# Attention's second product as 64 by 64 tiles, in batches of eight row groups

## The chip, the cores and the metric

The kernel runs on one core of a Trainium2 chip. The metric is the device time of one execution in microseconds (us), given as a median over runs. TensorE multiplies matrices into PSUM, a memory of eight banks; VectorE (DVE in the profile), ScalarE (ACT) and GpSimd (POOL) do elementwise work, POOL on SBUF alone in this kernel; SyncE (SP) issues most transfers.

## The reference

Two independent parts are computed, and their outputs stand side by side. Part A is a state-space layer (a complex linear recurrence over 2048 steps, with projections before and after). Part B is attention over segments of 32 tokens with a memory of 8 rows:

```python
for s in range(n_seg):                       # 64 segments of 32 tokens
    xs = x[:, s * seg_len:(s + 1) * seg_len, :].copy()
    h = jnp.concatenate([mem, xs], axis=1)   # 8 + 32 rows
    q, k, v = (jnp.einsum('btd,dhe->bhte', h, W) for W in (Wq, Wk, Wv))   # 32 heads of 128
    scores = jnp.einsum('bhqe,bhke->bhqk', q, k) * scale
    scores = jnp.where(mask[None, None], scores, -1000000000.0)
    p = _softmax(scores, axis=-1)
    o = jnp.einsum('bhqk,bhke->bhqe', p, v)
    o = jnp.einsum('bhte,hed->btd', o, Wo)
    mem = o[:, :M, :].copy()
    outs.append(o[:, M:, :])
```

The change is in the line that makes `o` from `p` and `v`, the second product.

## The kernel before

**Stages.** Projections of V and part A's recurrence come first, then part A's output, then the attention of part B (about 466 to 992 us in the profile), then the output projection. The memory rows of all segments are guessed ahead and checked at the end, so that the segments need no order.

**Attention.** The 2048 tokens are 16 groups of 128 rows, four segments in each. The 32 heads are worked in 16 head pairs (`hp`). A head pair has nine units: eight (`u` 0 to 7) of two groups each, and a small one (`NU`) for the first 40 rows with the true memory. At the start of a head pair `scores` computes all scores, transposed (keys on partitions), in 64 by 64 blocks: 64 matmuls of 128x64 tiles (L639) into four PSUM banks, one O buffer of two banks and both S buffers. PSUM is given out under three names of two buffers each: O (two banks a buffer), S and P (one bank a buffer).

`exps` turns one bank of scores into probabilities on ScalarE (L652). For each unit `att_front` multiplies two 64 by 64 blocks of each group by the causal mask on POOL (L663) into `mx`, a buffer of 128x128 tiles whose other blocks stay zero. Two units later `att_back` runs a quartet of matmuls, two groups by two heads (L704): the whole 128x128 tile of `mx` is the stationary operand and 129 columns of V (128 and a column of ones, which gives the sum of the softmax) move. VectorE adds the memory rows' share `b_u` (L706) and takes reciprocals (L708); POOL multiplies (L712) into `b_ot`, and after four units SP stores `b_ot` to DRAM in rows of 256 elements (L719, L720).

**What lies between.** Projections of Q and K for later head pairs fill TensorE: a head pair has 18 steps of `proj`, 16 of eight matmuls with 480 columns (L582) and two of sixteen with 136 (L593), with their casts on VectorE (L78) or ScalarE (L76). The main loop runs two steps a unit, 19 steps ahead. In the last head pair no projections are left, and steps of the output projection (`early`, L760) stand in. In the first head pairs, steps of `v_mem` project the memory rows' values (L484 on TensorE, sums at L511).

**What sets the order.** TensorE's order in attention follows the program, in which a unit, its projections and its exps are written out in `kernel_main`; the other engines' orders come from the compiled program, and PSUM buffers rotate, so that a matmul waits until the reader of its buffer two uses ago is done. SP's queue is in order: a store that waits for POOL holds back the loads behind it. V and `b_u` of a half (eight groups) are loaded into one of three buffers, about one head pair ahead (L606, L619).

Of the kernel before, what the change touches and what calls it, by code (L numbers as in the profile page):

```python
# [9 lines left out]
FP32 = mybir.dt.float32  # L10
# [3 lines left out]
ALU = mybir.AluOpType  # L14
# [79 lines left out]
def masks(k):  # L94

    G = k.G
    k.maskX = k.cst.tile([128, 128], BF16, name="maskX")
    k.maskM = k.cst.tile([128, L], BF16, name="maskM")
    G.memset(k.maskX[:], 0.0)
    G.memset(k.maskM[:], 0.0)  # L100
    for j in range(4):
        r = slice(32 * j, 32 * j + 32)
        G.memset(k.maskX[r, r], 1.0)
        G.affine_select(out=k.maskX[r, r], in_=k.maskX[r, r], compare_op=ALU.is_ge, fill=0.0, base=0,
                        pattern=[[1, 32]], channel_multiplier=-1)
    m = k.maskM[0:L, :]
    G.memset(m, 1.0)
    G.affine_select(out=m, in_=m, compare_op=ALU.is_ge, fill=0.0, base=0, pattern=[[1, L]], channel_multiplier=-1)
    G.memset(k.maskM[0:L, 0:M], 1.0)
# [185 lines left out]
class PartB:  # L295
# [219 lines left out]
    def qk_init(self, pool):  # L515
# [22 lines left out]
        for c in (0, VW - 1):  # L538
            G.memset(self.vs[:, :, c:c + 1], 1.0)
        self.ms = []  # L540
        self.mx, self.es, self.todo = [], {}, []
        for i in range(4):
            t = pool.tile([128, 4, 128], BF16, name=f"b_mx{i}", bufs=1)
            G.memset(t[:], 0.0)
            self.mx.append(t)
        for i in range(2):
            t = pool.tile([128, 2, 128], BF16, name=f"b_ms{i}", bufs=1)
            G.memset(t[:], 0.0)
# [62 lines left out]
    def load_u(self, i):  # L611
        if i < 2 * HP:
            k = self.k
            hp, half = divmod(i, 2)
            v = self.vt[hp // 2][:, :]
            for j in range(4):
                r = M - 1 + 32 * half + j
                src = bass.AP(v.tensor, v.offset + r * 512 + (hp % 2) * 256, [[0, 32], [4 * 512, NU], [1, 256]])
                d = k.SP.dma_start(self.ub[i % 3][32 * j:32 * j + 32, :, 1:257], src)  # L619
                if i < 3:  # L620
                    k.tc.keep_in_program_order(d)
# [7 lines left out]
    def scores(self, hp):  # L629
# [5 lines left out]
        for v in range(4):  # L635
            for j in range(8):
                g = M + (4 * v + j // 2) * 128
                for r in (0, 64):
                    k.tc.keep_in_program_order(k.PE.matmul(  # L639
                        banks[v][r:r + 64, j * 64:j * 64 + 64], kt[:, j % 2, g + r:g + r + 64], qt[:, j % 2, g + r:g + r + 64],  # L640
                        start=True, stop=True))
        self.todo = [(hp, v, banks[v]) for v in range(4)]
        self.exps()

    def exps(self):

        if self.todo:
            k = self.k
            hp, v, s = self.todo.pop(0)
            e = self.p3.tile([128, 512], BF16, name="b_e", bufs=4)  # L650
            i = hp * UPH + v
            k.S.activation(e[:], s, ACT.Exp, scale=float(E) ** -0.5, accum_out=self.accE[:, i:i + 1])  # L652
            self.es[2 * v], self.es[2 * v + 1] = (e[:, 256 * a:256 * a + 256] for a in range(2))

    def att_front(self, hp, u):
        k = self.k; PE = k.PE
        if u < NU:
            if u == 0:
                self.scores(hp)
            m = self.mx[u % 4]  # L660
            e = self.es.pop(u).rearrange("p (j q) -> p j q", j=4)
            for r in (slice(0, 64), slice(64, 128)):
                k.G.tensor_tensor(m[r, :, r], e[r], k.maskX[r, r].unsqueeze(1).to_broadcast([64, 4, 64]), ALU.mult)  # L663
            return m
        qt, kt = self.qk[hp % 2]
        s = k.ps("S")
        i = hp * UPH + u
        for hh in range(2):
            PE.matmul(s[:, hh * L:(hh + 1) * L], kt[:, hh, 0:128], qt[:, hh, 0:L], start=True, stop=True)
        e = self.p3.tile([128, 2 * L], BF16, name="b_es", bufs=1)  # L670
        k.S.activation(e[:], s[:, 0:2 * L], ACT.Exp, scale=float(E) ** -0.5, accum_out=self.accE[:, i:i + 1])
        m = self.ms[hp % 2]
        k.G.tensor_tensor(m[:, :, 0:L], e[:].rearrange("p (j q) -> p j q", j=2), k.maskM[:].unsqueeze(1).to_broadcast([128, 2, L]), ALU.mult)
        return m

    def att_back(self, hp, u, m):
        k = self.k; PE, V = k.PE, k.V
        o = k.ps("O")
        i = hp * UPH + u
        if u == NU:  # L680
            for hh in range(2):
                cs = slice(hh * 129, hh * 129 + 129)
                PE.matmul(o[:, 0, cs], m[:, hh, :], self.vs[:, hp % 2, cs], start=True, stop=True)
            r = self.rall[0:L, 4 * i:4 * i + 2]
            oa = o[0:L, 0, 0:VW]
            V.reciprocal(r, oa[:, 0:VW:VW - 1])
            if hp % 2 == 0:
                self.om = self.p3.tile([L, 2, 256], BF16, name="b_om", bufs=2)
            V.tensor_tensor(self.om[:, hp % 2, :].rearrange("p (h e) -> p h e", h=2), oa[:, 1:257].rearrange("p (h e) -> p h e", h=2),
                            r.unsqueeze(2).to_broadcast([L, 2, E]), ALU.mult)  # L690
            if hp % 2:
                hb = hp // 2
                cs = slice((hb % 2) * 512, (hb % 2) * 512 + 512)
                om = self.om[:].rearrange("p h n -> p (h n)")
                k.SP.dma_start(self.os[hb // 2][0:SEG, cs], om[M:L, :])
                k.SP.dma_start(self.omd[:, hb * 512:hb * 512 + 512], om[0:MT, :])
            return
        half, v = divmod(u, 4)
        b = (2 * hp + half) % 3
        vt, ut = self.vb[b], self.ub[b]  # L700
        for gg in range(2):
            for hh in range(2):
                cs = slice(hh * 129, hh * 129 + 129)
                PE.matmul(o[:, gg, cs], m[:, 2 * gg + hh, :], vt[:, 2 * v + gg, cs], start=True, stop=True)  # L704
        s = self.p3.tile([128, 2, VW], FP32, name="b_s", bufs=3)
        V.tensor_tensor(s[:], o[:, :, 0:VW], ut[:, 2 * v:2 * v + 2, :], ALU.add)  # L706
        r = self.rall[:, 4 * i:4 * i + 4].rearrange("p (a b) -> p a b", a=2)
        V.reciprocal(r, s[:, :, 0:VW:VW - 1])  # L708
        if v == 0:
            self.ot = self.p3.tile([128, NU, 256], BF16, name="b_ot", bufs=3)  # L710
        ot = self.ot
        k.G.tensor_tensor(ot[:, 2 * v:2 * v + 2, :].rearrange("p g (h e) -> p g h e", h=2),  # L712
                          s[:, :, 1:257].rearrange("p g (h e) -> p g h e", h=2),
                          r.unsqueeze(3).to_broadcast([128, 2, 2, E]), ALU.mult)
        if v == 3:
            os = self.os[hp // 4]
            cs = slice((hp % 4) * 256, (hp % 4) * 256 + 256)
            if half == 0:
                k.SP.dma_start(os[SEG:128, cs], ot[SEG:128, 0, :])  # L719
            k.SP.dma_start(os[1024 * half + 128 * (1 - half):1024 * half + 1024, cs].rearrange("(g p) n -> p g n", p=128), ot[:, 1 - half:NU, :])  # L720

    def attention(self):
        units = [(hp, u) for hp in range(HP) for u in (0, 1, 2, 3, NU, 4, 5, 6, 7)]
        pend = []
        for n, (hp, u) in enumerate(units):
            if u == 2:
                self.load_v(2 * hp + 2)
                self.load_u(2 * hp + 2)
            if u == 3 and hp % 2 == 0:
                self.load_vs(hp // 2)  # L730
            if u == 5:
                self.load_v(2 * hp + 3)
                self.load_u(2 * hp + 3)
            pend.append((hp, u, self.att_front(hp, u)))
            if len(pend) > 2:
                self.att_back(*pend.pop(0))
            yield hp, u
        for p in pend:
            self.att_back(*p)
            yield HP, 0  # L740


    def load_o(self, tb, q):
# [200 lines left out]
def kernel_main(tc, A_x, A_Lre, A_Lim, A_Bre, A_Bim, A_Cre, A_Cim, A_logdt, A_Dskip, B_x, B_mem0, B_Wq, B_Wk, B_Wv, B_Wo, out,  # L944
                force=False, dbg=None):
    with ExitStack() as ctx:
# [129 lines left out]
        with pool("p3", "right") as p3:  # L1076
# [19 lines left out]
            b.wo0, b.acc = [], {}  # L1096
            early = chain(b.op_some([(0, 0), (1, 0)], range(3), "P", 2), b.op_some([(2, 0), (3, 0)], range(3), "S", 2))
            for n, (hp, u) in enumerate(at):
                if u in (3, 5, 6) and hp < 7:
                    next(vms[hp + 1])  # L1100
                if u == 4 and hp < 6:
                    next(vms[hp + 2])
                if u == 4 and 8 <= hp < 12:
                    w = k.w8((8, 512), "wo0")
                    k.SP.dma_start(w, b.Wo[:, 8 * (hp - 8):8 * (hp - 7), 0:512])
                    b.wo0.append(w)
                if u == 6 and hp in (4, 8, 12):
                    b.load_o(0, hp // 4 - 1)
                want = min(18 * HP, 19 + 2 * (n + 1))
                if done == want:  # L1110
                    for _ in range(3 if u > 3 else 2):
                        next(early, None)
                for _ in range(2 if done == want else 0):
                    b.exps()
                while done < want:
                    next(pr)
                    b.exps()
                    done += 1
                    if done == 18 * HP:
                        w1 = xep.tile([128, KC, XP], BF16, name="b_xe")  # L1120
                        b.wo1 = w1[:].rearrange("p c n -> p (c n)")[:, 0:H * 512].rearrange("p (h n) -> p h n", h=H)
                        k.SP.dma_start(b.wo1, b.Wo[:, :, 512:D])
            for _ in early:
                pass

# [100 lines left out]
```

## Time and profile before

| what | value |
|---|---|
| median of 3 runs | 1199.17 us (1199.07 to 1200.29) |
| the profiled execution | 1199.58 us, span 1197.9 us |
| TensorE busy | 1192.0 us, 100% of the span |
| VectorE, ScalarE, POOL busy | 584.8, 346.3, 355.2 us |
| L704, second product | 512 matmuls, 51.0 us busy |
| L639, scores | 1024 matmuls |
| L663, masks on POOL | 256 instructions, 170.0 us |
| L706 and L708 on VectorE | 128 each, 88.5 and 22.8 us |
| L712, multiplies on POOL | 128 instructions, 133.0 us |

The granted clock of TensorE was full throughout. Busy times of matmuls overlap each other (each is drawn with its latency), so the time that a group takes from TensorE's stream is read from the starts of neighbours in the timeline. Idle time of other engines costs nothing while TensorE has work.

### The profile page before, as it was taken

The numbers are of one execution on the slowest core, as the hardware profiler recorded it, in microseconds if no ns is written. First come the engines' busy times: TensorE is split into PE (matmuls) and PEld (weight loads), VectorE is DVE, ScalarE is ACT, GpSimd is POOL, SyncE is SP. The second block draws the span as 40 slices with busy tenths as digits, with TensorE's granted clock in tenths as the row PEclk, the third lists the DMA queues.
The fourth block names the chain that finished last, engine by engine and source line by source line (L and its number), as shares of the span: only waits on it lengthen the run. The fifth ranks groups of instructions, "written<-read, shape, count | busy, mean of one in ns | idle before, by whom it ended". The sixth has DMA issues, their size and how long they took to land.

```text
span 1197.9 us, 20039 instructions
## 1 busy us (share of the span) xinstructions
PE 1192.0 (100%) x8104; PEld 608.9 (51%) x8104; DVE 584.8 (49%) x1004; ACT 346.3 (29%) x713; POOL 355.2 (30%) x484
## 2 busy tenths in 40 slices
PE   9999999999999999999999999999999999999998
PEld 4444444444445544555555555555555554444444
DVE  4889999999982333244344444444444432100000
ACT  3344344443420002334433343333333310000000
POOL 1000000000012332355555666666666671000000
PEclk9999999999999999999999999999999999999999
DMA  9941332322656732988789776855585478807000
GB/s 239 269 126 55 96 105 63 97 84 66 148 178 200 230 103 62 222 209 175 179 179 214 174 177 146 175 134 137 136 169 132 98 214 194 202 18 158 18 27 20
DMA packets 333873, 168.50 MB, mean 141 GB/s; under 512 B 144512, under 2 KB 327608, under 8 KB 333760
## 3 DMA queue, kind: packets, MB, share of 16 engines
q1 hardware_dynamic: 331696, 165.33, 56.5%
q10 hardware_dynamic: 2080, 1.84, 0.5%
q8 instruction: 65, 1.06, 0.4%
q14 instruction: 32, 0.26, 0.1%
HBM read 89.74 MB, written 43.70 MB: 111 GB/s over the span
## 4 chain that ended last, share of the span: by engine, by line
PE 98%; POOL 1%; issue 0%; DVE 0%; ACT 0%; POOLq 0%; ACTq 0%
PE psP L582 35%; PE psS L760 10%; PE psS L386 9%; PE psP L386 9%; PE psO L234 9%; PE psS L288 5%; PE psP L288 5%; PE psP L760 4%; PE psP L593 3%; PE psO L704 3%; PE psO L760 2%; PE psS L793 1%; PE psO L639 1%; PE psP L484 1%; POOL b_mx L663 1%; PE psS L639 1%
## 5 line engine op out<-in xcount | busy, mean ns | idle before, releaser
L582 PE MATMUL psP<-b_xe,w 128*128 128x480 bf16 x2048 | 435.9, 366 | 0.0
L582 PEld LDWEIGHTS <-w 128*128 128x128 bf16 x2048 | 194.2, 98 | 186.1
L663 POOL TENSOR_TENSOR b_mx<-b_e,maskX 64x256 bf16<-64x256 bf16 x256 | 170.0, 664 | 96.1 <-ACT b_e L652 53.8
L78 DVE CAST b_q<-psP 128x480 bf16<-128x480 f32 (+2 forms) x160 | 92.2, 585 | 203.5 <-PE psP L582 134.3
L712 POOL TENSOR_TENSOR b_ot<-b_s,b_rall 128x512 bf16<-128x512 f32 x128 | 133.0, 1039 | 118.3 <-DVE b_rall L708 111.5
L283 POOL TENSOR_TENSOR a_xd<-a_xn,b_wide 128x512 f32<-128x512 bf16 x32 | 36.8, 1152 | 418.4 <-DMA a_xn<-in_A_x_dram 350.8
L386 PEld LDWEIGHTS <-b_xe 128*128 128x128 bf16 x1024 | 99.8, 98 | 119.1 <-DVE b_xe L78 0.3
L760 PEld LDWEIGHTS <-b_ol 128*128 128x128 bf16 x960 | 93.4, 98 | 110.3
L76 ACT ACTIVATE b_k<-psP 128x480 bf16<-128x480 f32 x128 | 72.7, 568 | 252.3 <-PE psP L582 248.4
L706 DVE TENSOR_TENSOR b_s<-psO,b_u 128x516 f32<-128x516 f32 x128 | 88.5, 692 | 100.3 <-PE psO L704 81.9
L234 PE MATMUL psO<-w,a_bt 128*128 128x512 bf16 x512 | 115.7, 379 | 0.0
L760 PE MATMUL psS<-w,b_ol 128*128 128x512 bf16 x416 | 92.9, 379 | 0.0
L386 PE MATMUL psS<-w,b_xe 128*128 128x512 bf16 x384 | 90.7, 379 | 0.0
L386 PE MATMUL psP<-w,b_xe 128*128 128x512 bf16 x384 | 90.7, 379 | 0.0
L234 PEld LDWEIGHTS <-a_bt 128*128 128x128 bf16 x512 | 49.7, 98 | 59.0
L288 PEld LDWEIGHTS <-a_hs 128*128 128x128 bf16 x512 | 49.5, 98 | 58.3
L78 DVE CAST b_ost<-psS 128x512 bf16<-128x512 f32 x13 | 9.0, 691 | 138.6 <-PE psS L760 138.6
L565 ACT ACTIVATE b_wide<-w 128x1024 bf16<-128x1024 bf16 x64 | 67.6, 1056 | 0.5
L76 ACT ACTIVATE b_vst<-psS 128x512 bf16<-128x512 f32 x56 | 33.4, 597 | 96.1 <-PE psS L386 80.3
L288 PE MATMUL psS<-w,a_hs 128*128 128x512 bf16 x256 | 57.9, 379 | 0.0
L288 PE MATMUL psP<-w,a_hs 128*128 128x512 bf16 x256 | 57.9, 379 | 0.0
L76 ACT ACTIVATE b_vst<-psP 128x512 bf16<-128x512 f32 x56 | 33.4, 597 | 83.8 <-PE psP L386 77.7
(205 smaller groups left out, 1107.5 us busy)
## 6 DMA issues: line engine op xcount, KB each, us to landing
b_v<-b_vx SPq DMA_DIRECT2D x32, 512.0 KB
b_u<-b_vt SPq DMA_DIRECT2D x128, 128.0 KB
b_vx<-b_vst SPq DMA_DIRECT2D x56, 256.0 KB
w<-in_B_Wv_dram SPq DMA_DIRECT2D x14, 1024.0 KB
w<-in_B_Wo_dram SPq DMA_DIRECT2D x12, 1024.0 KB
w<-in_B_Wq_dram SPq DMA_DIRECT2D x16, 512.0 KB
w<-in_B_Wk_dram SPq DMA_DIRECT2D x16, 512.0 KB
b_os<-b_ot SPq DMA_DIRECT2D x16, 512.0 KB
```

The lines of the kernel that those rows point to most:

```text
L76: self.S.activation(out, in_, ACT.Copy)
L78: self.V.tensor_copy(out, in_)
L234: m = PE.matmul(u[:, i, :], self.bt[:, i, c, :], self.xT[tb][:, c, :], start=(c == 0), stop=(c == KC - 1))
L283: G.tensor_tensor(xd[:], xn[:], dB[:, hs], ALU.mult)
L288: PE.matmul(py[:], self.hs[tb][:, pc, i, tt * 128:(tt + 1) * 128], self.ct[half, i][:, pc, :], start=(pc == 0 and i == 0), stop=(pc == PC ...
L386: m = self.k.PE.matmul(p[:], self.xe[:, c, t * 128:(t + 1) * 128], w[:, c, :], start=(c == 0), stop=(c == KC - 1))
L565: k.tc.keep_in_program_order(k.S.activation(wide, w[:, i * KC:(i + 1) * KC, hh * 128:(hh + 1) * 128], ACT.Square, accum_out=self.nrm[:, n: ...
L582: PE.matmul(p[:, 0:480], w[:, i * KC + c, hh * 128:(hh + 1) * 128], self.xe[:, c, 480 * q:480 * q + 480], start=(c == 0), stop=(c == KC - 1))
L663: k.G.tensor_tensor(m[r, :, r], e[r], k.maskX[r, r].unsqueeze(1).to_broadcast([64, 4, 64]), ALU.mult)
L706: V.tensor_tensor(s[:], o[:, :, 0:VW], ut[:, 2 * v:2 * v + 2, :], ALU.add)
L712: k.G.tensor_tensor(ot[:, 2 * v:2 * v + 2, :].rearrange("p g (h e) -> p g h e", h=2), s[:, :, 1:257].rearrange("p g (h e) -> p g h e", h=2 ...
L760: k.PE.matmul(self.acc[t, half], ol[:, h8, tt * 128:(tt + 1) * 128], self.wo_half(half, h), start=(h == 0), stop=(h == H - 1))
```

## The change

The second product uses 64 by 64 tiles of TensorE, four at a time: two row halves (keys) by two column halves (queries, that is, PSUM partitions). Four groups give the lower 64 output partitions and four the upper, so that eight groups, a half of the sequence, form one batch of 32 matmuls in `values`. It writes six PSUM banks: both O buffers and both S buffers, with the two row halves in different banks. The probabilities stay compact: they are masked in place, one POOL instruction of 128x512 for each bank of scores, and `mx` goes. `norm3` and `norm1` add, take reciprocals and multiply, for six and two blocks of 64 rows at a time; they and the later exps are put in a list, from which `tick` takes one after each projection step. The output rows lie in another order on the partitions, and the store and the load of `b_u` are rearranged to match. The head pair's units run 0 to 8 with the batches in units 3 and 7 and the small unit in 4 and 6; loads and `v_mem` steps move to other units.

```diff
 def masks(k):
-    k.maskX = k.cst.tile([128, 128], BF16, name="maskX")
+    k.maskX = k.cst.tile([128, 64], BF16, name="maskX")
...
     def load_u(self, i):
-                r = M - 1 + 32 * half + j
-                src = bass.AP(v.tensor, v.offset + r * 512 + (hp % 2) * 256, [[0, 32], [4 * 512, NU], [1, 256]])
+                r = M - 1 + 32 * half + 16 * (j // 2) + j % 2
+                src = bass.AP(v.tensor, v.offset + r * 512 + (hp % 2) * 256, [[0, 32], [2 * 512, NU], [1, 256]])
...
     def scores(self, hp):
-        self.todo = [(hp, v, banks[v]) for v in range(4)]
-        self.exps()
+        self.exp(hp, 0, banks[0])
+        self.todo += [(self.exp, hp, v, banks[v]) for v in range(1, 4)]
...
+    def exp(self, hp, v, s):
...
+        k.S.activation(e[:], s, ACT.Exp, scale=float(E) ** -0.5, accum_out=self.accE[:, i:i + 1])
+        ev = self.es[v] = e[:].rearrange("p (j q) -> p j q", j=8)
+        k.G.tensor_tensor(ev, ev, k.maskX[:].unsqueeze(1).to_broadcast([128, 8, 64]), ALU.mult)
...
-            m = self.mx[u % 4]
-            e = self.es.pop(u).rearrange("p (j q) -> p j q", j=4)
-            for r in (slice(0, 64), slice(64, 128)):
-                k.G.tensor_tensor(m[r, :, r], e[r], k.maskX[r, r].unsqueeze(1).to_broadcast([64, 4, 64]), ALU.mult)
...
-        for gg in range(2):
-            for hh in range(2):
-                PE.matmul(o[:, gg, cs], m[:, 2 * gg + hh, :], vt[:, 2 * v + gg, cs], start=True, stop=True)
-        s = self.p3.tile([128, 2, VW], FP32, name="b_s", bufs=3)
-        V.tensor_tensor(s[:], o[:, :, 0:VW], ut[:, 2 * v:2 * v + 2, :], ALU.add)
...
+    def values(self, hp, half):
...
+        vt = self.vb[(2 * hp + half) % 3]
+        o = [k.ps("O") for i in range(2)]
+        sp = [k.ps("S") for i in range(2)]
+        for v, hh in [(v, hh) for hh in range(2) for v in range(3)] + [(3, 0), (3, 1)]:
+            cs = slice(hh * 129, hh * 129 + 129)
+            for i in range(2):
+                e = self.es[2 * half + i]
+                ph = slice(64 * i, 64 * i + 64)
+                for b in range(2):
+                    r = slice(64 * b, 64 * b + 64)
+                    out = sp[b][ph, cs] if v == 3 else o[hh][ph, b, v * 129:v * 129 + 129]
+                    k.tc.keep_in_program_order(k.PE.matmul(
+                        out, e[r, 2 * v + hh, :], vt[r, 4 * i + v, cs], start=True, stop=True))
+        self.ot = self.p3.tile([128, NU, 256], BF16, name="b_ot", bufs=3)
+        self.norm3(hp, half, 0, o[0])
+        self.todo += [(self.norm3, hp, half, 1, o[1]), (self.norm1, hp, half, 0, sp[0]), (self.norm1, hp, half, 1, sp[1])]
...
+    def norm3(self, hp, half, hh, o):
...
+        s = self.p3.tile([128, 2, 3, 129], FP32, name="b_s", bufs=3)
+        k.V.tensor_tensor(s[:], o[:, :, 0:387].rearrange("p b (v n) -> p b v n", v=3),
+                          four(self.ub[(2 * hp + half) % 3])[:, :, :, hh * 129:hh * 129 + 129], ALU.add)
...
+        k.V.reciprocal(r, s[:, :, :, 128 * hh])
+        k.G.tensor_tensor(four(self.ot)[:, :, :, hh * E:hh * E + E], s[:, :, :, 1 - hh:1 - hh + E],
+                          r.unsqueeze(3).to_broadcast([128, 2, 3, E]), ALU.mult)
+    def norm1(self, hp, half, b, sp):
...
+        V.tensor_tensor(s[:, b, :], sp[:, 0:VW], self.ub[(2 * hp + half) % 3][:, 6 + b, :], ALU.add)
+        if b == 0:
+            return
...
+        os = self.os[hp // 4][1024 * half:1024 * half + 1024, (hp % 4) * 256:(hp % 4) * 256 + 256]
+        os = os.rearrange("(i w p) n -> i p w n", i=2, w=NU)
+        if half:
+            k.SP.dma_start(os[0], self.ot[0:64])
+        else:
+            k.SP.dma_start(os[0, SEG:64, 0, :], self.ot[SEG:64, 0, :])
+            k.SP.dma_start(os[0, :, 1:NU, :], self.ot[0:64, 1:NU, :])
+        k.SP.dma_start(os[1], self.ot[64:128])
...
     def attention(self):
-        units = [(hp, u) for hp in range(HP) for u in (0, 1, 2, 3, NU, 4, 5, 6, 7)]
...
+                if u in (3, 7):
+                    self.values(hp, u // 4)
+                if u == 4:
+                    self.small_front(hp)
+                if u == 6:
+                    self.small_back(hp)
+                yield hp, u
...
-                if u in (3, 5, 6) and hp < 7:
+                if u in (2, 4, 6) and hp < 7:
                     next(vms[hp + 1])
...
                 if done == want:
-                    for _ in range(3 if u > 3 else 2):
-                        next(early, None)
+                    for i in range(2):
+                        if i < (2, 1, 0, 2, 1, 2, 0, 2, 2)[u]:
+                            next(early, None)
+                        b.tick()
                 while done < want:
                     next(pr)
-                    b.exps()
+                    b.tick()
```

## Prediction

> **What bounds the kernel now.** I read the page first (engine totals, the chain that ended last), then TensorE's timeline inside one head pair of the attention stage, then the groups by form for the instructions that the change touches, and last the timeline around the one stall.
>
> ```profile
> PE 1192.0 (100%) x8104; PEld 608.9 (51%) x8104; DVE 584.8 (49%) x1004; ACT 346.3 (29%) x713; POOL 355.2 (30%) x484
> PE 98%; POOL 1%; issue 0%; DVE 0%; ACT 0%; POOLq 0%; ACTq 0%
> ```
>
> TensorE is the whole chain, and every other engine is busy half of the span or less. So only two things can move the end: the time that TensorE's own stream takes, and any new wait in that stream. The stream itself, two units of the head pair that starts at 720 us:
>
> ```profile
> 716.22 1.11 PE L593 MATMUL psP<-b_xe,w 128*128 128x136 bf16 x16
> 717.17 0.40 PE L704 MATMUL psO<-b_v,b_mx 128*128 128x129 bf16 x4
> 717.41 1.11 PE L593 MATMUL psP<-b_xe,w 128*128 128x136 bf16 x16
> 718.35 1.78 PE L582 MATMUL psP<-b_xe,w 128*128 128x480 bf16 x8
> 720.07 0.70 PE L639 MATMUL psO<-b_q,b_k 128*64 128x64 bf16 x32
> 720.59 0.67 PE L639 MATMUL psS<-b_q,b_k 128*64 128x64 bf16 x32
> 721.20 0.41 PE L704 MATMUL psO<-b_v,b_mx 128*128 128x129 bf16 x4
> 721.45 3.40 PE L582 MATMUL psP<-b_xe,w 128*128 128x480 bf16 x16
> 724.68 0.40 PE L704 MATMUL psO<-b_v,b_mx 128*128 128x129 bf16 x4
> 724.92 1.38 PE L582 MATMUL psP<-b_xe,w 128*128 128x480 bf16 x6
> ```
>
> Read starts, not durations, which overlap. Four L704 matmuls (second product) occupy the stream from 724.68 to 724.92, 0.24 us, 59 ns each, hidden by nothing. Sixteen L582 take 724.68 − 721.45 = 3.23 us, 202 ns each. So eight L582 from 718.35 should let the next work in at 719.97, but the 128x64 score tiles start at 720.07: changing the tile shape costs 0.10 us. The first 32 scores take 0.52 us (16 ns each, because two column tiles stream at once); the next 32 take 0.61 until L704 starts, 0.09 more: the price of changing back. The only other stall of the stage is in the last head pair:
>
> ```profile
> 982.58 0.29 PE L683 MATMUL psO<-b_vs,b_ms 128*128 128x129 bf16 x2 [0.56 <-POOL b_ms L673]
> ```
>
> **The second product on TensorE.** Removed: 128 quartets. At 0.236 us each (the mean of their starts in the trace, 0.247 behind scores) that is 128 x 0.236 + 16 x 0.01 = 30.4 us. Added: 1024 matmuls of 64x64 tiles with 129 columns, in 32 batches of 32. A batch is eight rounds of four tiles: two row halves that write different banks, by two column halves. No row shows a row-tiled matmul, so the round is bounded from both sides. Below: 59 ns, the rate of one 129-column matmul, if four tiles stream at no extra cost. Above, if they do stream together: 4 x 16 = 65 ns, the rate at which scores issue. Starts of the score pairs lie 31.6 ns apart, of which 26.7 is 64 columns, so a small extra per round exists; I take 62. Each batch also pays 0.10 + 0.09 for two changes of shape and, as scores do, 0.017 for the first round's weights: 8 x 0.062 + 0.21 = 0.70 us. 32 batches are 22.5 us; in the last head pair the compiled order splits one batch around two output matmuls, 0.2 more. Sum 22.7, a gain of 7.7 us (8.5 at 59 ns, 6.9 at 65).
>
> Two rules of the Trainium skill speak against this. Row: 32 scores in 0.52 us, 16 ns start to start. Rule ("TensorE: Matmul & The Clock Gate", section "Wait — 56ns, not 53.3ns?"): starts are never closer than about 25 ns. By the rule 1024 x 25 = 25.6 us plus 33 x 0.2 us is 32.2 us, 1.8 us slower; by the row, the gain above. The row is this kernel's own column tiles, so I go by it. Second row: the same scores load a new 64-column weight tile for each matmul inside those 16 ns. Rules: column tiling switches the fast weight load off ("TensorEngine Tiling (Array Packing)", "Restrictions"), and a load takes columns / 1.2 ns ("TensorE: Matmul & The Clock Gate", "LDWEIGHTS"), 53 ns for 64. Four such loads one after another make a round of 213 ns and the batches 61 us; the scores show that loads of different column tiles overlap and hide, so I keep 62 ns and leave a serial version to the first rival.
>
> **What TensorE waits for.** The order of the compiled programs is the same up to the first scores. In a head pair it becomes: scores, then nine units of two projections, with one batch ahead of the fourth unit's projections and one ahead of the eighth's. Probabilities: the four exps run back to back after the scores (0.59 us apart in the trace, from 0.8 us after they start), and the first batch comes about 10 us later, so POOL's masks are covered. PSUM: the batch takes six banks (both two-bank O buffers, both S buffers), free since exps and the small unit left them units before. The next scores need the S banks 5.1 us after the second batch (3.5 and one L582 set of 1.62), when the chain below is over.
>
> The tight place is VectorE after the second batch. The compiled order puts all seven normalisation instructions ahead of the casts of the two narrow projections:
>
> ```profile
> L706 DVE TENSOR_TENSOR b_s<-psO,b_u 128x516 f32<-128x516 f32 x126 | 87.1, 692 | 98.2 <-PE psO L704 79.8 <-PE psS L511 7.5 <-DMA b_u<-b_vt 5.0
> L708 DVE RECIPROCAL b_rall<-b_s 128x4 f32<-128x4 f32 x126 | 22.5, 178 | 4.1
> L241 DVE TENSOR_TENSOR a_a<-psO,a_cs 128x1024 f32<-128x1024 f32 x32 | 39.0, 1218 | 11.1 <-PE psO L234 11.0
> 717.37 0.51 DVE L78 CAST b_q<-psP 128x256 bf16<-128x256 f32 x2 [1.65 <-PE psP L593]
> ```
>
> From 516 and 1024 elements: 1.035 ns an element. So a 774-element add is 0.96 us, a 258-element one 0.425. Chain: 2 x 0.96 + 2 x 0.425 + 3 x 0.178 + casts 0.51 = 3.8 us end to end; independent neighbours overlap by 0.08 in the trace, five of them, 3.4. It starts 0.15 us before the batch ends (its first bank pair is done after three of eight rounds) and so ends 3.25 us behind it. TensorE wants that P bank after one L582 set and two L593 sets: 1.62 + 2 x 0.95 = 3.52 us. Margin about 0.25 us; cost taken 0. Without overlap it is about 0.15 late, 15 times, 2 us.
>
> **Other edits.** All beside TensorE:
>
> ```profile
> L663 POOL TENSOR_TENSOR b_mx<-b_e,maskX 64x256 bf16<-64x256 bf16 x256 | 170.0, 664 | 96.1 <-ACT b_e L652 53.8 <-PE psO L704 21.2 <-ACT b_es L671 8.4
> L712 POOL TENSOR_TENSOR b_ot<-b_s,b_rall 128x512 bf16<-128x512 f32 x128 | 133.0, 1039 | 118.3 <-DVE b_rall L708 111.5
> L283 POOL TENSOR_TENSOR a_xd<-a_xn,b_wide 128x512 f32<-128x512 bf16 x32 | 36.8, 1152 | 418.4 <-DMA a_xn<-in_A_x_dram 350.8 <-DVE a_ot L290 67.5
> ```
>
> POOL's masks go from 256 halves to 64 of 128x512, at L283's 1.15 us: 170 to 74 us. Its multiplies keep their elements: 64 of 768 at about 1.5 and 32 of 512 at 1.04, 130 us. VectorE's adds: 64 x 0.96 + 64 x 0.425 = 89 against 88.5, 32 fewer reciprocals. ACT keeps its exps. Stores of b_ot go from 3 to 5 a head pair, 0.38 us of SP's queue each (32 more, 12 us over 500), with the same bytes; behind them wait loads of b_u and the Q/K weights that are used tens of us later. Loads of b_u and b_v are issued one or no unit earlier and used three units later than before: cover grows. The first projections' rows and bytes do not change. The v_mem steps move by a unit and their results serve later head pairs; only their sums on TensorE (L511 now) wait for a POOL product that stands behind the first batch's multiplies, about 7 us after the batch, and they come 10 us after it. None is on the path; if that cover were gone, the stores would cost up to 12 us.
>
> **The last head pair.** With no projection to fill, output matmuls (216 ns) do. By the compiled order: the second mask is ready 0.2 us after the batch wants it; the small unit's scores, only eight output matmuls (1.73 us) behind the first batch, wait some 0.4 us for VectorE to free an S bank; its product waits 0.3 for POOL. About 0.9 us, in place of the 0.7 stall (0.56 shown) of now: 0.2 lost.
>
> **The sum.** 7.7 − 0.2 = 7.5 us. The profiled execution took 1199.6 (span 1197.9 and 1.7 around it), so 1192.1 on its own basis. It was 0.4 above the median 1199.17 of the runs; on that basis 1191.7.
>
> **The rivals.** *Row halves do not stream together* (the side of slower). Two row tiles of one column half deliver into the same PSUM partitions, or their weight loads queue. Place: each round; price: two streams, 124 ns, so a batch costs 1.20 and the 32 cost 38.6 us, 8.2 more than now; with the tail 1207.6. It decides from a round of about 90 ns, where 32 x (0.72 + 0.21) + 0.2 reaches what the quartets cost less the tail. For it: no row of the trace has row tiles. Against: column tiles overlap fully, and the banks differ. *VectorE is late after the second batch*: strided three-run adds at 1.2 us instead of 0.96 lengthen the chain by 0.5, 0.2 to 0.3 us stall x 15, about 4 us: 1195.5. For: the margin is only 0.25. Against: TENSOR_TENSOR follows the element count in both rows. *The gain is larger*: 59 ns and no tail loss, 1190.5.
>
> **How the numbers follow.** Forecast as told 0.68, VectorE late 0.14, row halves serial 0.12, larger gain 0.06. A measurement of this kernel tells about 0.2% (2.4 us) from no change. Faster: forecast, larger gain and most of VectorE late, 0.84; within: the rest of VectorE late and partly serial rounds, 0.04; slower 0.12. The range goes from 1189.7 (59 ns, cheaper changes of shape) to 1196.0 (VectorE late); it leaves out the serial case.
>
> **What would show it.** Right: 1024 values matmuls with starts advancing 62 ns per four; batches taking 0.70 us out of the stream; score batches 30.6 us apart where they are 31.1 now; POOL near 257 us busy; no TensorE wait on VectorE in front of the projections that follow the narrow ones. Wrong: rounds near 120 ns, or a gap at that place in every head pair.

## The result, and the profile after

The changed kernel takes 1192.5 us (median of four runs; 1192.0 to 1193.3) where the kernel before took 1199.15 beside it: ratio 0.9943, 95% interval 0.9926 to 0.9960. Forecast were 1191.7 us, and 1192.1 on the basis of a profiled execution; the profiled one took 1192.41, span 1190.7. The page's first line after:

```profile
PE 1180.4 (99%) x8547; PEld 591.8 (50%) x8616; DVE 570.1 (48%) x972; ACT 346.9 (29%) x713; POOL 249.3 (21%) x256
```

TensorE is still busy throughout. Of its 8616 matmuls (one for each weight load, PEld) 69 have no record; the chain that ended last reaches back only to 970 us in this trace, so it is not used here. TensorE's timeline around the second batch of a head pair, the counterpart of the stretch shown for before (columns: start, length, engine, line, operation, output and inputs, tile, shape, count):

```profile
891.26 3.40 PE L579 MATMUL psP<-b_xe,w 128*128 128x480 bf16 x16
894.59 0.54 PE L706 MATMUL psO<-b_v,b_e 64*64 64x129 bf16 x24
894.95 0.29 PE L706 MATMUL psS<-b_v,b_e 64*64 64x129 bf16 x8
895.17 1.79 PE L579 MATMUL psP<-b_xe,w 128*128 128x480 bf16 x8
896.80 2.06 PE L590 MATMUL psP<-b_xe,w 128*128 128x136 bf16 x32
898.70 1.78 PE L579 MATMUL psP<-b_xe,w 128*128 128x480 bf16 x8
900.41 0.69 PE L636 MATMUL psO<-b_q,b_k 128*64 128x64 bf16 x32
900.94 0.67 PE L636 MATMUL psS<-b_q,b_k 128*64 128x64 bf16 x32
```

Sixteen L579 (L582 before) from 891.26 would let the next work in at 894.49; the batch starts at 894.59, 0.10 us for the change of shape, and the projections go on at 895.17. So a batch with its entry takes 0.68 us, for eight groups, where four quartets took 4 x 0.236 = 0.94. Some 0.02 us more is lost in the starts of other projections: summed from start to start over one head pair, the 64 small matmuls take 1.17 us and the 128 wide projections 26.23, in place of 26.00 before. A batch thus takes (1.17 + 0.23) / 2 = 0.70 us out of the stream, and eight quartets took 1.90. The narrow projections L590 (L593 before) start at 896.80, and the next projection at 898.70 is where 32 x 59 ns puts it: no wait. VectorE in the same stretch:

```profile
895.06 1.83 DVE L717 TENSOR_TENSOR b_s<-psO,b_u 128x774 f32<-128x774 f32 x2 [1.33 <-PE psO L706]
...
897.74 0.18 DVE L736 RECIPROCAL b_rall<-b_s 128x4 f32<-128x4 f32 x1
897.95 0.51 DVE L78 CAST b_q<-psP 128x256 bf16<-128x256 f32 x2
```

The casts of `b_q`, which free the P bank, end at 898.46 (897.95 + 0.51), 0.24 us before TensorE starts the projection that takes it. And the groups by form on POOL and VectorE, which answer to the masks, multiplies and adds of before:

```profile
L722 POOL TENSOR_TENSOR b_ot<-b_s,b_rall 128x768 bf16<-128x768 f32 x64 | 93.2, 1478 | 261.0 <-issue 133.2 <-DVE b_rall L721 127.8
L655 POOL TENSOR_TENSOR b_e<-b_e,maskX 128x512 bf16<-128x512 bf16 x64 | 71.9, 1155 | 42.2 <-ACT b_e L653 42.2
L717 DVE TENSOR_TENSOR b_s<-psO,b_u 128x774 f32<-128x774 f32 x64 | 58.7, 959 | 44.6 <-PE psO L706 30.5 <-POOL b_e L655 4.4 <-DMA b_omd<-b_om 2.7
L731 DVE TENSOR_TENSOR b_s<-psS,b_u 128x258 f32<-128x258 f32 x64 | 24.9, 389 | 0.0
```

What was not as forecast is the last head pair, in TensorE's timeline:

```profile
959.99 0.69 PE L636 MATMUL psO<-b_q,b_k 128*64 128x64 bf16 x32
960.51 0.68 PE L636 MATMUL psS<-b_q,b_k 128*64 128x64 bf16 x32
961.12 2.76 PE L789 MATMUL psP<-w,b_ol 128*128 128x512 bf16 x11
963.81 0.24 PE L706 MATMUL psO<-b_v,b_e 64*64 64x129 bf16 x2
964.51 0.53 PE L706 MATMUL psO<-b_v,b_e 64*64 64x129 bf16 x22 [0.45 <-POOL b_e L655]
...
967.26 0.20 PE L664 MATMUL psS<-b_q,b_k 128*128 128x40 bf16 x2 [0.48 <-DVE b_s L731]
...
970.24 0.29 PE L677 MATMUL psO<-b_vs,b_ms 128*128 128x129 bf16 x2 [0.18 <-POOL b_ms L668]
```

The bracket gives idle time after the modelled end of the matmul before it. From start to start the delay is larger: the first batch loses 0.69 us after its second matmul (963.81 to 964.51), the small scores (L664) about 0.43 and their product (L677) 0.35. The counts show missing records: the eleven L789 from 961.12 to 963.81 must be twelve, at 216 ns each. Such gaps are not counted as waiting. That is 1.5 us in place of one 0.7 us stall before.

### The profile page after: what moved, and what is told of

The parts are those of the page before. It is cut to its first block, busy times and chain, and to the rows that moved or that the text cites. A ratio compares the mean times of both kernels' runs of the same rounds, so it can differ in the third digit from the quotient of the medians.

```text
span 1190.7 us, 20609 instructions
## 1 busy us (share of the span) xinstructions
PE 1180.4 (99%) x8547; PEld 591.8 (50%) x8616; DVE 570.1 (48%) x972; ACT 346.9 (29%) x713; POOL 249.3 (21%) x256
## 5 line engine op out<-in xcount | busy, mean ns | idle before, releaser
L579 PE MATMUL psP<-b_xe,w 128*128 128x480 bf16 x2048 | 429.2, 366 | 0.0
L579 PEld LDWEIGHTS <-w 128*128 128x128 bf16 x2048 | 193.4, 98 | 197.3
L789 PEld LDWEIGHTS <-b_ol 128*128 128x128 bf16 x960 | 93.3, 98 | 112.2 <-issue 0.2
L722 POOL TENSOR_TENSOR b_ot<-b_s,b_rall 128x768 bf16<-128x768 f32 x64 | 93.2, 1478 | 261.0 <-issue 133.2
L789 PE MATMUL psS<-w,b_ol 128*128 128x512 bf16 x407 | 91.6, 379 | 0.4
L655 POOL TENSOR_TENSOR b_e<-b_e,maskX 128x512 bf16<-128x512 bf16 x64 | 71.9, 1155 | 42.2 <-ACT b_e L653 42.2
L717 DVE TENSOR_TENSOR b_s<-psO,b_u 128x774 f32<-128x774 f32 x64 | 58.7, 959 | 44.6 <-PE psO L706 30.5
```

The lines of the kernel that those rows point to most:

```text
L579: PE.matmul(p[:, 0:480], w[:, i * KC + c, hh * 128:(hh + 1) * 128], self.xe[:, c, 480 * q:480 * q + 480], start=(c == 0), stop=(c == KC - 1))
L655: k.G.tensor_tensor(ev, ev, k.maskX[:].unsqueeze(1).to_broadcast([128, 8, 64]), ALU.mult)
L717: k.V.tensor_tensor(s[:], o[:, :, 0:387].rearrange("p b (v n) -> p b v n", v=3), four(self.ub[(2 * hp + half) % 3])[:, :, :, hh * 129:hh * ...
L722: k.G.tensor_tensor(four(self.ot)[:, :, :, hh * E:hh * E + E], s[:, :, :, 1 - hh:1 - hh + E], r.unsqueeze(3).to_broadcast([128, 2, 3, E]), ...
L789: k.PE.matmul(self.acc[t, half], ol[:, h8, tt * 128:(tt + 1) * 128], self.wo_half(half, h), start=(h == 0), stop=(h == H - 1))
```

## The experiments

The theory: the gain is TensorE's stream alone, because four small tiles stream at once; each batch pays for two changes of tile shape; nothing else matters until the last head pair, where late masks and a late PSUM buffer cost 1.5 us in place of 0.7. Rivals: small tiles are cheap by themselves; the row halves do not stream together; POOL's relief is part of the gain; VectorE's margin is not real.

**Issue order of the batch.** Three kernels issue the same 32 matmuls in another order. In the changed kernel `i` (column half) and `b` (row half) run innermost. The three orders stand here as comments, with `vh` for the list of `(v, hh)`.

```diff
-        for v, hh in [(v, hh) for hh in range(2) for v in range(3)] + [(3, 0), (3, 1)]:
-            for i in range(2):
-                for b in range(2):
+        # tile by tile:  for i in range(2): for b in range(2): for v, hh in vh
+        # row pairs:     for i in range(2): for v, hh in vh: for b in range(2)
+        # column pairs:  for b in range(2): for v, hh in vh: for i in range(2)
```

Tile by tile:

> The same 32 matmuls of a batch, issued tile by tile: eight in a row on each 64x64 tile. If the gain comes from four tiles that stream at once, nothing is left to stream together: 32 x 59 ns and about 0.21 us for the changes of shape, 2.1 us a batch in place of 0.68, 32 x 1.4 = 45 us more than the changed kernel, about 1237 us. If instead small tiles were cheap by themselves (a rival: fewer rows and columns to fill), the time would stay near 1192.5 us.

Measured: 1217.0 us, ratio to before 1.0147 (1.0130 to 1.0164), 24.5 us above the changed kernel. The direction is as expected, so small tiles are not cheap by themselves, but the size is half. The timeline of one batch says why:

```profile
573.65 0.56 PE L707 MATMUL psO<-b_v,b_e 64*64 64x129 bf16 x8
574.02 0.22 PE L707 MATMUL psS<-b_v,b_e 64*64 64x129 bf16 x1
574.05 0.21 PE L707 MATMUL psO<-b_v,b_e 64*64 64x129 bf16 x1
574.08 0.22 PE L707 MATMUL psS<-b_v,b_e 64*64 64x129 bf16 x1
574.10 0.36 PE L707 MATMUL psO<-b_v,b_e 64*64 64x129 bf16 x5
...
575.00 2.20 PE L579 MATMUL psP<-b_xe,w 128*128 128x480 bf16 x10
```

The program has six psO and then two psS on each tile, and it fixes the order of issue. The trace shows eight psO first and then psS and psO in turn. By the single starts, the next tile's first matmul begins 6 ns after the fifth of the tile in hand, while three of that tile have not begun; its second and third slip in between those three. Once running, matmuls of one tile start 56 to 61 ns apart, whatever the other tile does. So matmuls of a free tile start ahead of up to three that were issued earlier. (The order in TensorE's queue itself is not in the trace.) The batch takes 575.00 − 573.65 + 0.10 = 1.45 us in place of my 2.1; 32 x (1.45 − 0.68) = 24.6 us, which is the time measured.

Row pairs and column pairs:

> The same matmuls, with the column halves one after the other: neighbours in the order differ in the row half alone. If row halves stream together as column halves do, 16 pairs of about 59 ns: 0.95 + 0.21 = 1.16 us a batch, 32 x 0.48 = 15 us more, about 1208 us. If the row halves do not stream together (the first rival of the prediction), this is as slow as tile by tile, about 1237 us.

> The same matmuls, with the row halves one after the other: neighbours differ in the column half alone, as the scores' do. 16 pairs of about 59 ns, 1.16 us a batch, about 1208 us by every theory; a difference to the row pairs says which direction of the array costs more.

Measured: 1201.1 us both (ratios to before 1.0013, 1.0004 to 1.0023, and 1.0015, 1.0005 to 1.0025). Batch of the row pairs, and then of the column pairs:

```profile
571.84 0.56 PE L707 MATMUL psO<-b_v,b_e 64*64 64x129 bf16 x16
...
572.68 3.41 PE L579 MATMUL psP<-b_xe,w 128*128 128x480 bf16 x16
```

```profile
571.42 0.56 PE L707 MATMUL psO<-b_v,b_e 64*64 64x129 bf16 x16
...
572.27 3.41 PE L579 MATMUL psP<-b_xe,w 128*128 128x480 bf16 x16
```

Both occupy 0.84 us and 0.10 to enter, 0.94: what four quartets of the old tile cost, so pairs alone gain nothing. The row halves stream together as well as the column halves, and the prediction's first rival falls. They are 7 us faster than I expected, for the most part by what was seen tile by tile: by the single starts, the second half's first pair begins while three pairs of the first half have not, some 0.2 us early, 32 times.

**The price of changing the shape.**

```diff
         for v, hh in [(v, hh) for hh in range(2) for v in range(3)] + [(3, 0), (3, 1)]:
             cs = slice(hh * 129, hh * 129 + 129)
+            if (v, hh) == (1, 1):
+                k.tc.keep_in_program_order(k.PE.matmul(sp[0][:, 400:401], k.ident[:], k.ident[:, 0:1], start=True, stop=True))
```

> One matmul of a full 128x128 tile with a single column is put between the fourth and the fifth round of each batch; its result is not used. By my sum a change of shape and back is 0.19 us, with the first round's weights and its own issue 0.24 us, 32 times: 7.7 us more, about 1200 us, so the whole gain of the change is gone. A rival, that tiles of different shapes follow each other freely and the 0.1 us steps seen at the scores are bank waits of theirs, gives 32 x 0.03 = 1 us more, about 1193.5 us.

Measured: 1199.4 us, ratio to before 1.0001 (0.9992 to 1.0011).

```profile
571.21 0.42 PE L708 MATMUL psO<-b_v,b_e 64*64 64x129 bf16 x16
571.56 0.18 PE L701 MATMUL psS<-ident 128*128 128x1 bf16 x1
571.67 0.31 PE L708 MATMUL psO<-b_v,b_e 64*64 64x129 bf16 x8
...
572.03 3.42 PE L579 MATMUL psP<-b_xe,w 128*128 128x480 bf16 x16
```

One single-column matmul of the full tile costs 6.9 us in all. It is 0.23 us a batch (0.82 us from the batch's start to the projections, 0.59 without it) for the 30 batches ahead of the last head pair; that pair loses nothing (226.07 us from its scores to the last matmul in both traces), and there the waits are shorter: the first batch loses 0.46 us to the late mask in place of 0.69. The theory holds; the batch of eight groups is what makes the small tiles pay. Two batches of four groups would, by this figure, cost the same second change, and the gain would be gone; such a kernel was not run.

**VectorE's margin.** In the second batch of each head pair the second large add is done twice (lines shortened).

```diff
-        k.V.tensor_tensor(s[:], o[:, :, 0:387]..., ALU.add)
+        for _ in range(2 if half and hh else 1):
+            k.V.tensor_tensor(s[:], o[:, :, 0:387]..., ALU.add)
```

> In the second batch of each head pair VectorE runs the second 774-element add twice (the same values, written again), 0.88 us more ahead of the casts of the narrow projections. In the changed kernel those casts end 0.23 us before TensorE wants the bank. If that margin is what keeps TensorE free there, the wait is 0.88 - 0.23 = 0.65 us in most of 15 head pairs: 7 to 10 us more, 1199.5 to 1202.5 us, the gain gone. If VectorE does not matter (a rival: the wait falls elsewhere or buffers absorb it), the time stays near 1192.5 us.

Measured: 1199.0 us, 6.5 us more (ratio to before 0.9996, 0.9987 to 1.0006). TensorE now waits at the place named:

```profile
901.84 2.06 PE L590 MATMUL psP<-b_xe,w 128*128 128x136 bf16 x32
904.17 1.17 PE L579 MATMUL psP<-b_xe,w 128*128 128x480 bf16 x5 [0.28 <-DVE b_rall L737]
```

904.17 − 901.84 = 2.33 us, where 1.90 is the work of the 32: 0.43 late. The place exists in 14 head pairs (in the fifteenth the last scores follow the narrow projections at once), and there it is 0.34 or 0.43 us late, 5.6 us in all; the other 0.6 of the 6.2 us between the two traces is spread over the end of the attention and one other head pair. The margin is real, and it is small. Not all of the 0.24 us is slack: here TensorE starts 0.06 to 0.15 us after the casts of `b_q` end, so by an estimate a chain on VectorE that is 0.1 to 0.2 us longer than its 3.4 us now would begin to cost. The wait is smaller than I expected, and the trace shows one reason: the compiler put these casts ahead of the last reciprocal.

**POOL's relief.** Each mask is multiplied in twice.

```diff
-        k.G.tensor_tensor(ev, ev, k.maskX[:].unsqueeze(1).to_broadcast([128, 8, 64]), ALU.mult)
+        for _ in range(2):
+            k.G.tensor_tensor(ev, ev, k.maskX[:].unsqueeze(1).to_broadcast([128, 8, 64]), ALU.mult)
```

> Every mask multiply on POOL is done twice (a mask of ones and zeros changes nothing the second time), 74 us more POOL work, so POOL is about as busy as in the kernel before. If POOL's relief has no part in the gain, nothing changes in 15 head pairs, and only the last, where masks come late, grows: its first batch waits for two more masks, 2 x 1.15 = 2.3 us, and the small unit's for about 1 more, so about 1195.5 us. If POOL's relief were part of the gain, each head pair would lose some of it, and the period of the score batches would rise above 30.6 us.

Measured: 1197.1 us (ratio to before 0.9980, 0.9971 to 0.9990), 4.5 us more. The score batches still come 30.60 us apart in the later head pairs, as in the changed kernel, so POOL's relief has no part in the gain there. The loss is in the last head pair: from the start of its scores to the kernel's last matmul the trace has 230.3 us, and 226.1 in the changed kernel.

```profile
962.29 9.15 POOL L656 TENSOR_TENSOR b_e<-b_e,maskX 128x512 bf16<-128x512 bf16 x8
964.73 0.24 PE L707 MATMUL psO<-b_v,b_e 64*64 64x129 bf16 x2 [0.69 <-POOL b_e L656]
968.05 0.53 PE L707 MATMUL psO<-b_v,b_e 64*64 64x129 bf16 x22 [3.08 <-POOL b_e L656]
```

The rest of the first batch is 3.4 us later against the scores than in the changed kernel (968.05 against 964.51, with the scores 0.15 later). That is three mask multiplies of 1.15 and not two: it starts as the fifth of the eight ends (968.00), where I had counted four. Why it needs the fifth is not shown; a compiled order in which the third mask's first multiply comes before the second mask's last would do it.

**The waits of the last head pair.** First the masks of that pair alone go to VectorE; then also the small unit's mask, and its scores go to an O buffer (lines shortened).

```diff
+        eng = k.V if hp == HP - 1 else k.G
-        k.G.tensor_tensor(ev, ev, ...)
+        eng.tensor_tensor(ev, ev, ...)
... second kernel, in small_front:
-        s = k.ps("S")
+        s = k.ps("O")[:, 0, :] if hp == HP - 1 else k.ps("S")
-        k.G.tensor_tensor(m[:, :, 0:L], ...)
+        eng.tensor_tensor(m[:, :, 0:L], ...)
```

> In the last head pair alone the four masks go to VectorE, which is idle there. By my reading of the trace POOL is still busy with the multiplies of the pair before (until 2.2 us after the scores start), so the first batch's second mask comes late and TensorE waits 0.69 us. With VectorE this wait goes: 1191.8 us. The waits behind it (0.65 for an S bank, 0.35 for the small unit's mask) stay or move earlier as they are. If the first batch waited for something else (its values or the exps), no change.

> As the kernel with VectorE's masks in the last head pair, and there also the small unit's mask on VectorE and its scores in an O buffer, which is free 1.4 us before the S bank. This takes away the causes of all three waits of the last head pair, 0.69 + 0.65 + 0.35 = 1.7 us: about 1190.8 us, the fastest version. If one of the waits only moves to the next user (the end of the second batch to the S banks of the output matmuls), about 1191.5.

Measured: 1192.35 us for the masks alone (0.9941, 0.9928 to 0.9955) and 1191.1 for all of it (0.9931, 0.9918 to 0.9945). With the masks moved, the batch runs without a break (all 24 psO from 963.65) and the other two waits stay; with all moved none of the three is left:

```profile
964.31 0.54 PE L708 MATMUL psO<-b_v,b_e 64*64 64x129 bf16 x24
964.67 0.29 PE L708 MATMUL psS<-b_v,b_e 64*64 64x129 bf16 x8
964.89 1.68 PE L791 MATMUL psP<-w,b_ol 128*128 128x512 bf16 x7
966.63 0.21 PE L665 MATMUL psO<-b_q,b_k 128*128 128x40 bf16 x2
966.68 2.75 PE L791 MATMUL psP<-w,b_ol 128*128 128x512 bf16 x12
969.27 0.28 PE L679 MATMUL psO<-b_vs,b_ms 128*128 128x129 bf16 x2
```

From the start of the last scores to the last matmul the traces have 226.07 us for the changed kernel, 225.44 and 224.59 for these two: the masks are worth 0.63 us, and all of it 1.48, which is the sum of the three waits as measured (a larger sum in an expectation still counted missing records as waiting). In its median the first step cannot be told from the changed kernel (1191.8 to 1192.8 against 1192.0 to 1193.3), so the traces alone show it. The start of the kernel differs by as much from execution to execution: the first scores of the three profiles come at 494.86, 495.02 and 495.51. So the changed kernel and the last version ran once more side by side:

> The changed kernel once more, on the same chip and beside the same runs of the kernel before as the next one: 1192.5 us, within 0.3.

> The kernel without the three waits of the last head pair, beside the changed kernel on one chip: 1.2 to 1.7 us less than it, near 1191.1 us; the waits that it takes out add up to 1.7. If its earlier time was luck of the chip, the two agree within 0.4 us.

Measured: 1192.46 (1192.20 to 1192.84) and 1191.08 (1190.91 to 1191.59): 1.4 us apart, without overlap. This version beats both kernels.

## Why the prediction was right, point by point

- *The four tiles stream at once.* Right, in both directions of the array. Rounds start 57.5 ns apart in the mean (55 to 61; 81 for the first), where I took 62 from bounds of 59 and 65. My lower bound was not one: a matmul of 129 columns takes 59 ns in the full tile and 57.5 in a 64x64 tile. The small extra per round was reckoned from 26.7 ns for 64 columns, which follows from two groups of before: L582 and L593 start 202.5 and 59.1 ns apart, and (202.5 − 59.1) / (480 − 136) = 0.417 ns a column. Shorter rounds cancel against a dearer first round and way out, so that the batch takes 0.70 us as forecast; that they cancel so well is luck.
- *The shape's price.* Right: 0.10 to enter, and 0.23 for one more change and back when measured by itself.
- *The gain of the batches.* Right: 30.4 − 32 x 0.70 − 0.2 = 7.8 us, where 7.7 were told. The periods show it; two score batches in a row before (the first of them, at 720.07, stands in the prediction) and after:

```profile
751.16 0.69 PE L639 MATMUL psO<-b_q,b_k 128*64 128x64 bf16 x32
...
716.82 0.69 PE L636 MATMUL psO<-b_q,b_k 128*64 128x64 bf16 x32
...
747.42 0.69 PE L636 MATMUL psO<-b_q,b_k 128*64 128x64 bf16 x32
```

  The later score batches are 31.09 us apart before and 30.60 after (30.6 forecast); the difference is 8 x 0.236 + 0.01 − 2 x 0.70 = 0.50 by the sum and 0.49 in the traces.
- *The rule of a 25 ns floor* (the Trainium skill, "TensorE: Matmul & The Clock Gate", section "Wait — 56ns, not 53.3ns?") did not hold for matmuls of different tiles: the four of a round start 3 to 4 ns apart, and a round takes 57.5 ns, 14 a matmul. Nor was there a serial load of weights: the four loads of a round start 3 to 4 ns apart as well.
- *VectorE after the second batch.* Right by a margin of 0.24 us, forecast 0.25. The adds took 959 ns, forecast 0.96, and 389 in place of 425.
- *POOL, stores, loads.* Hidden, as told; POOL is 249 us busy in place of 257. That twice the masks cost nothing outside the last pair shows it for POOL. The two added stores of a head pair were not tried alone; no wait of TensorE in the attention ends on a transfer in the trace after. (Before, SP's queue stood 107 us in 32 waits of stores for `b_ot`, at no cost to TensorE.)
- *The last head pair* is the term that was mis-sized: 1.5 us of waits in place of 0.9, a loss of 0.75 and not 0.2. The small scores (0.4 forecast, 0.43) and their product (0.3, 0.35) were right; the first wait was 0.69 in place of 0.2. The step that failed is "the second mask is ready 0.2 us after the batch wants it". The prediction names no work of POOL ahead of these masks. In the trace they stand behind the multiplies of the head pair before, 0.8 us after the first exp is done (961.38):

```profile
960.78 0.60 ACT L653 ACTIVATE b_e<-psO 128x512 bf16<-128x512 f32 x1 [2.01 <-PE psO L636]
...
958.32 2.91 POOL L722 TENSOR_TENSOR b_ot<-b_s,b_rall 128x768 bf16<-128x768 f32 x2 [9.66 <-issue]
961.20 1.04 POOL L738 TENSOR_TENSOR b_ot<-b_s,b_rall 128x512 bf16<-128x512 f32 x1
962.19 4.49 POOL L655 TENSOR_TENSOR b_e<-b_e,maskX 128x512 bf16<-128x512 bf16 x4
```

  In other head pairs another projection of 1.62 us stands between the second batch and the scores, and 10 us of projections stand between the scores and the first batch; here the first is missing, and only 2.7 us of output matmuls take the place of the second. Moving the masks took the 0.69 away, and moving the small unit's buffer and mask took the other two.
- *The sum.* From the first scores to the last matmul the traces have 697.9 us before and 691.0 after, 6.9 us, where 7.8 − 0.75 gives 7.0. Told were 7.5; the 0.6 between is the last head pair's 0.55. The span fell by 7.2 us (1197.9 to 1190.7); 0.24 of the other 0.3 is that the first scores came earlier (495.02 in place of 495.26). That is chance: the profiles of the other runs, with nothing changed ahead of the attention, have 494.86 to 495.51. In the medians the miss is 0.8 us; what goes beyond the last head pair is within the difference between executions (the profiled one of before lay 0.4 above its median, that of after 0.1 below).

## What to carry to other kernels

Where TensorE has no gaps, the gain of an edit is the change in the starts of its stream, read from the timeline around the edit, and a small-tile batch has to be long enough to pay 0.2 us for going in and out of its shape. Then look for the place where the usual cover is missing, here the last pass of the loop: trace the queue of each engine there from what the pass before left on it, not from an empty queue. A few instructions moved to an idle engine, and one buffer exchanged, in that pass alone gave back 1.4 us here.

## What the runs showed that I had not expected

Matmuls for different tiles did not start in program order: tile by tile, the next tile's first matmul started 6 ns after the fifth of the eight of the tile in hand, ahead of three that the program has before it. It makes a poor order cheaper (1.45 us a batch and not 2.1) without making it good (0.68). And pairs of 64x64 tiles, whether rows or columns, cost 0.94 us for eight groups, the same as the full tile with half of its cells idle.
